# Two decode attentions on one core: VectorE and ScalarE programs as loops over chunk pairs, B's output weights loaded straight into one small buffer

## The chip, the cores and the metric

One core of one Trainium2 chip. The metric is device microseconds of one execution. The changed kernel and the kernel before were run alternately on one chip; executions of one kernel agree within about 0.2%.

## The reference, cut to what matters

```python
# two problems, A and B; 4 sequences, one query each, head size 128, bf16
# A: 32 query heads share 8 key/value heads; the last 2048 keys count
# B: 32 heads with keys and values of their own; 8192 keys
def ref(x, k_cache, v_cache, wq, wo):
    q = (x @ wq).reshape(B, Sq, H, Dh).transpose(0, 2, 1, 3)
    scores = einsum("bhqd,bhkd->bhqk", q, k) * Dh ** -0.5
    o = einsum("bhqk,bhkd->bhqd", softmax(scores), v)
    return o.transpose(0, 2, 1, 3).reshape(B, Sq, H * Dh) @ wo
# out = concatenate([A, B], -1)
```

Every key and value is used once: 587 MB come from memory, nine tenths of them B's.

## The kernel before

Work is cut into 8 chunks of A (2 MB of keys, 2 MB of values) and 64 of B (one sequence, two heads: 4 MB of keys, 4 MB of values). For each chunk PE transposes the keys in groups of 8 tiles, DVE and ACT copy them out of PSUM, PE multiplies them with the query, then softmax and the product with the values follow. SP issues all loads, in order. A small scheduler writes a list of operations for each engine; only PE's list is turned into a loop over pairs of B chunks, with waits against `i * step + value`.

```python
def emit_looped(self, engname, eng, sems, loop):
    a, b, steps = self.periods()              # where PE's list repeats
    self.emit_ops(pe[:m[a]], eng, sems)
    with loop(0, b - a) as i:
        self.emit_ops(pe[m[a]:m[a + 1]], eng, sems,
                      lambda sname, val: i * steps[sname] + val if steps[sname] else val)
    self.emit_ops(pe[m[b]:], eng, sems)
# ... (cut)
@block.tensor                                  # PE: a loop
def _(e): sch.emit_looped("pe", e, sems, loop)
@block.vector                                  # DVE and ACT: every instruction written out
def _(e): sch.emit("dve", e, sems)
@block.scalar
def _(e): sch.emit("act", e, sems)
# ... (cut) output weights: 512 KB (4 heads) into one of three slots; DVE copies the 2 heads in use
def dma_wo(i):
    dst = wor[:, slot, :].rearrange("p (hl n) -> p hl n", hl=4)
    sch.add_dma("sp", lambda e: e.dma_start(dst, src), "d_wo%d" % slot, waits=waits, key=("wo", i))
def emit_wos(c):
    sch.add("dve", lambda e: e.tensor_copy(wos[:, :, :], w[:, h:h + 2, :]), ...)
```

PE needs the same operands in each turn of its loop, hence the small copy `wos`.

## Time and profile before

| | before |
|---|---|
| time, median of 6 runs | 1386.33 us (1384.96 to 1387.15) |
| read from memory | 587.2 MB, 424 GB/s over the span, 431 in the steady stage |
| busy PE, DVE, ACT | 85%, 46%, 31% of the span |
| PE's wait for keys | 169 us in 61 waits |
| instructions run; written out for PE, DVE, ACT | 57,099; 3453, 1328, 526 |

### The profile page before, as it was taken

To read this page: it belongs to the slowest core of one execution; us is meant where nothing else is said; L and a number is where in the kernel's file an instruction comes from. 1 tells how busy PE (TensorE), PEld (TensorE's weight loads), DVE (VectorE), ACT (ScalarE), POOL (GpSimd) and SP (SyncE) were. 2 spreads that over 40 slices of the span, in tenths; PEclk is the share of its full clock that TensorE was granted. 3 is DMA by queue.
4 is the path that set the end of the run, shared out by engine and by line. 5 is a ranking of instruction groups with operands and counts; after the bars stand their busy time and mean duration, and the time that the engine had idled before them with its cause. 6 is when DMAs were issued, how large, how long until landed. Compare 5 with 4: busy or idle time off the path is not lost.

```text
span 1384.5 us, 57099 instructions
## 1 busy us (share of the span) xinstructions
PE 1173.0 (85%) x26769; PEld 1130.0 (82%) x26769; DVE 643.2 (46%) x1326; ACT 436.1 (31%) x649; POOL 4.1 (0%) x14
## 2 busy tenths in 40 slices
PE   4888888898888788988889788888898888888888
PEld 4777878897888788887889788887798888887887
DVE  1566444454444444444444444444454445444443
ACT  1554323333223322332233233332233233322332
POOL 1000000000000000000000000000000000000000
PEclk9899999999999999999999999999999999999998
DMA  9999999999999999999999999999999999999996
GB/s 400 414 417 422 426 428 430 434 425 437 427 436 427 432 430 434 429 425 436 427 436 427 435 427 436 426 428 435 429 434 430 433 427 435 428 429 432 431 434 255
DMA packets 29979, 587.80 MB, mean 425 GB/s; under 512 B 2656, under 2 KB 10864, under 8 KB 11120
## 3 DMA queue, kind: packets, MB, share of 16 engines
q1 hardware_dynamic: 29912, 587.22, 99.2%
q8 instruction: 27, 0.44, 0.1%
q14 instruction: 16, 0.13, 0.0%
q10 hardware_dynamic: 24, 0.01, 0.0%
HBM read 587.21 MB, written 0.01 MB: 424 GB/s over the span
## 4 chain that ended last, share of the span: by engine, by line
DMA 66%; PE 31%; DVE 1%; issue 1%; ACT 0%; SPq 0%; ACTq 0%; DVEq 0%
DMA kv<-in_B_k_cache_dram 64%; PE tr L321 19%; PE sc L323 9%; DMA kv<-in_B_wq_dram 2%; PE fin L323 2%; PE po L323 1%; PE ms L323 1%; DVE sA L430 1%; DVE kt L383 0%; DVE rm L439 0%; DVE sA L428 0%; ACT pba L493 0%; PE ms L321 0%; ACT kt L381 0%; ACT pbb L478 0%
## 5 line engine op out<-in xcount | busy, mean ns | idle before, releaser
L321 PE MATMUL tr<-identb,kv 128*128 128x128 bf16 x8704 | 702.7, 231 | 171.7 <-DMA kv<-in_B_k_cache_dram 169.0
L383 DVE COPY kt<-tr 128x1024 bf16<-128x1024 bf16 x736 | 502.6, 691 | 484.5 <-PE tr L321 480.4
L321 PEld LDWEIGHTS tr<-identb,kv 128*128 128x128 bf16 x8704 | 557.7, 105 | 197.4 <-issue 128.6
L381 ACT ACTIVATE kt<-tr 128x1024 bf16<-128x1024 bf16 x352 | 360.2, 1024 | 638.1 <-PE tr L321 635.0
L323 PE MATMUL sc<-qb,kt 128*128 128x64 bf16 x8192 | 424.6, 197 | 1.7 <-issue 1.5
L323 PEld LDWEIGHTS sc<-qb,kt 128*128 128x128 bf16 x8192 | 350.8, 101 | 3.9 <-issue 1.6
L323 PE MATMUL po<-pbb,kv 128*128 128x64 bf16 (+1 forms) x8192 | 289.9, 192 | 5.5 <-issue 5.5
L323 PEld LDWEIGHTS po<-pbb,kv 128*128 128x128 bf16 x8192 | 263.3, 97 | 7.6 <-issue 5.8
L478 ACT ACTIVATE pbb<-sc,negb 64x128 bf16<-64x128 f32 x128 | 51.2, 400 | 296.8 <-DVE negb L468 296.0
L444 DVE TENSOR_REDUCE rm<-sc 64x1 f32<-64x128 f32 x128 | 37.0, 289 | 94.2 <-PE sc L323 93.3
L456 DVE TENSOR_REDUCE gm<-ms 1x2 f32<-1x128 f32 (+1 forms) x72 | 20.1, 279 | 44.6 <-PE ms L321 44.5
L468 DVE COPY negb<-ms 128x1 f32<-128x1 f32 (+1 forms) x72 | 11.4, 159 | 55.4 <-PE ms L323 55.4
L323 PE MATMUL sc<-qs,kt 128*128 128x64 bf16 (+3 forms) x512 | 26.6, 198 | 10.8 <-DVE kt L383 10.5
L323 PEld LDWEIGHTS sc<-qs,kt 128*128 128x128 bf16 x512 | 21.8, 102 | 13.2 <-DVE kt L383 11.8
L323 PE MATMUL ms<-identf,gx 1*128 1x1 f32 (+1 forms) x144 | 27.8, 260 | 0.6 <-DVE gx L460 0.6
L323 PEld LDWEIGHTS ms<-identf,gx 1*128 1x128 f32 (+1 forms) x144 | 21.7, 188 | 4.9 <-DVE gx L460 0.8
L478 ACT ACTIVATION_READ_ACCUMULATOR pbb<-sc,negb 64x1 f32 x128 | 23.7, 185 | 0.0
L321 PE MATMUL ms<-identf,rm 128*1 128x128 f32 (+1 forms) x72 | 19.8, 275 | 0.2 <-DVE rm L444 0.2
L323 PE MATMUL fin<-wos,oz 128*4 128x512 bf16 x64 | 19.5, 386 | 0.3 <-DVE oz L542 0.3
L323 PE MATMUL po<-pba,kv 128*128 128x64 bf16 x512 | 18.9, 193 | 0.0
L460 DVE TENSOR_SCALAR gx<-gm 1x128 f32<-1x128 f32 (+1 forms) x72 | 15.9, 221 | 2.5
L323 PEld LDWEIGHTS po<-pba,kv 128*128 128x128 bf16 x512 | 16.6, 98 | 0.0
(47 smaller groups left out, 155.5 us busy)
## 6 DMA issues: line engine op xcount, KB each, us to landing
kv<-in_B_k_cache_dram SPq DMA_DIRECT2D x64, 4096.0 KB, 27.7
kv<-in_B_v_cache_dram SPq DMA_DIRECT2D x63, 4096.0 KB, 32.5
kv<-in_A_k_cache_dram SPq DMA_DIRECT2D x8, 2048.0 KB, 27.4
kv<-in_A_v_cache_dram SPq DMA_DIRECT2D x8, 2048.0 KB, 26.6
kv<-in_A_wq_dram SPq DMA_DIRECT2D x1, 4096.0 KB, 12.3
kv<-in_B_wq_dram SPq DMA_DIRECT2D x1, 4096.0 KB, 27.3
wor<-in_A_wo_dram SPq DMA_DIRECT2D x8, 512.0 KB, 23.6
wor<-in_B_wo_dram SPq DMA_DIRECT2D x8, 512.0 KB, 33.6
```

The costliest lines, as they stand in the source:

```text
L321: emit = lambda e: e.transpose(o, l, r)
L323: emit = lambda e: e.matmul(o, l, r, start=start, stop=stop)
L381: sch.add("act", lambda e: e.activation(dst, src, ACTF.Copy), waits=waits, key=("ev", s))
L383: sch.add("dve", lambda e: e.tensor_copy(dst, src), waits=waits, key=("ev", s))
L430: emit = lambda e, src=src, b=b: e.scalar_tensor_tensor(out=t, in0=src, scalar=mk[:, b:b + 1], in1=t, op0=ALU.mult, op1=ALU.add)
L444: sch.add("dve", lambda e, src=src, pp=pp: e.tensor_reduce(out=rm[pp, m, 0:1], in_=src, axis=AX.X, op=ALU.max), waits=[("S", ch["s_last"]) ...
L456: sch.add("dve", lambda e: e.tensor_reduce(out=gm[0:C, m, 0:U], in_=src, axis=AX.X, op=ALU.max), waits=[("trm", c)], key=("gmax", c))
L460: sch.add("dve", lambda e: e.tensor_scalar(out=dst, in0=gv, scalar1=-scale, scalar2=None, op0=ALU.mult), waits=[("gmax", c)], key=("gx", c))
L468: sch.add("dve", lambda e: e.tensor_copy(negb[:, m, 0:C], ms[:, col:col + C]), waits=[("bc", c)], key=("negb", c))
L478: sch.add("act", lambda e, src=src, pp=pp, n=n, u=u: e.activation(pbv[pp, :, u], src, ACTF.Exp, bias=negb[pp, m, 0:1], scale=scale, accum_ ...
```

## The change: intent and diff

The intent: shorter VectorE and ScalarE programs (1328 to 295 and 526 to 122 instructions written out), by the same loop that PE has. A loop's turns must be alike, which the three slots and the alternating masks of before were not. So B's output weights now go by DMA straight into `wos`, 256 KB for each head pair, and a mask multiplication replaces the two result buffers.

```diff
-        rz = sb("rz", [P, 2, 8], F32)
+        rz = sb("rz", [P, 8], F32)
+        pm = sb("pm", [P, HB // 2, 2, 2, 4], F32)          # 0/1 masks for the two pairs of a head pair
@@
+        def dma_wos(hp):
+            src = B_wo[2 * hp * P:2 * (hp + 1) * P, :].rearrange("(hl d) n -> d hl n", d=P)
+            sch.add_dma("sp", lambda e: e.dma_start(wos[:, :, :], src), "d_wos",
+                        waits=[("fin", NCA + 4 * hp - 1)] if hp else [], key=("wos", hp))
@@ SP's list
+            if kind == "k" and c >= NCA and (c - NCA) % 4 == 3:
+                dma_wos((c - NCA) // 4)
             dma_kv(kind, c)
+            if kind == "v" and c > NCA + 2 and (c - NCA) % 2 == 1:
+                sch.add("sp", lambda e: e.sem_inc(sems["eng_sp"], 1), waits=[("wos", (c - NCA - 2) // 4)], ...)
@@ after the reciprocal of a B pair
+                sch.add("dve", lambda e, x=0: e.tensor_tensor(out=rz..., in0=bcast(ri, ...),
+                    in1=pv[:, bass.ds(x + pair, 8)]..., op=ALU.mult), waits=[("rinv", c), "c_pm"], ...)
@@
-        def emit_wos(c): ...                                # the copy on DVE
@@ output product of a pair
-                if c > NCA + 2 and (c - NCA) % 2 == 1 and g == 4:
+                if c > NCA + 2 and (c - NCA) % 2 == 1 and g == 10:
                     emit_fin(c - 2)
@@
-            sch.emit("dve", e, sems)
+            sch.emit_looped("dve", e, sems, loop_on(mybir.EngineType.DVE, 0), 1)
-            sch.emit("act", e, sems)
+            sch.emit_looped("act", e, sems, loop_on(mybir.EngineType.Activation, 0), 1)
```

(Cut: the search for the period for each engine, and addresses that advance with the turn.)

More of the change, by code (lines that the diff above doesn't have):

```diff
@@ L25, with __getattr__, call, of @@
 TRM0, BC0, L0, Q0, XT0 = 0, 256, 288, 320, 448
+class _Record:
+    def __getattr__(self, name):
+        def call(*args, **kw):
+            return (name,) + tuple(self.of(x) for x in args) + tuple((k, self.of(kw[k])) for k in sorted(kw))
+        return call
+    @staticmethod
+    def of(x):
+        if isinstance(x, bass.AP):
+            return x.tensor.name, x.offset, str(x.ap), str(x.dtype)
+        return str(x)
 class _Sched:
@@ L36, in __init__, with add @@
         self.marks = []
-    def add(self, eng, emit, waits=(), key=None, what=None):
+    def add(self, eng, emit, waits=(), key=None, at=None, self_inc=False):
         sig = None
@@ L44, in add @@
             self.tk[key] = ("eng_" + eng, self.count[eng])
-        self.ops[eng].append((emit, tuple(waits), sig, what))
+        self.ops[eng].append((emit, tuple(waits), None if self_inc else sig, at))
     def add_dma(self, eng, emit, semname, waits=(), key=None):
@@ L55, in mark @@
     def mark(self):
-        self.marks.append(len(self.ops["pe"]))
+        self.marks.append({n: len(self.ops[n]) for n in self.ops})
     def needs(self, waits):
@@ L65, in needs, with emit_ops @@
         return need
-    def emit_ops(self, ops, eng, sems, value=lambda sname, val: val):
+    def emit_ops(self, ops, eng, sems, step=None, count=None):
         waited = {}
-        for emit, waits, sig, _ in ops:
+        for k, (emit, waits, sig, at) in enumerate(ops):
             for sname, val in self.needs(waits).items():
@@ L72, in emit_ops @@
                     continue
-                eng.wait_ge(sems[sname], value(sname, val))
+                by = step[sname] if step else 0
+                eng.wait_ge(sems[sname], count * by + val if by else val)
                 waited[sname] = val
-            ins = emit(eng)
+            if at is None:
+                ins = emit(eng)
+            else:
+                ins = emit(eng, count * step[k] if step else 0)
             if sig is not None:
@@ L80, in emit, with periods @@
         self.emit_ops(self.ops[engname], eng, sems)
-    def periods(self):
-        pe, best = self.ops["pe"], (0, 0, {})
-        for a in range(len(self.marks) - 1):
-            steps, b = {}, a
-            first = pe[self.marks[a]:self.marks[a + 1]]
-            while b + 1 < len(self.marks):
-                this = pe[self.marks[b]:self.marks[b + 1]]
-                if len(this) != len(first) or any(x[2:] != y[2:] for x, y in zip(first, this)):
-                    break
-                fine = True
-                for x, y in zip(first, this):
-                    nx, ny = self.needs(x[1]), self.needs(y[1])
-                    fine = fine and set(nx) == set(ny)
-                    for sname in set(nx) & set(ny):
-                        if b > a:
-                            fine = fine and ny[sname] - nx[sname] == (b - a) * steps.setdefault(sname, (ny[sname] - nx[sname]) // (b - a))
+    def periods(self, engname, pairs):
+        ops, marks = self.ops[engname], [m[engname] for m in self.marks]
+        rec = _Record()
+        says = [(emit(rec) if at is None else emit(rec, -at), sig) for emit, _, sig, at in ops]
+        best = (0, 0, {})
+        for a in range(len(marks) - pairs):
+            w0, w1 = marks[a], marks[a + pairs]
+            n, step = 1, {}
+            while a + (n + 1) * pairs < len(marks):
+                v0, v1 = marks[a + n * pairs], marks[a + (n + 1) * pairs]
+                fine = says[w0:w1] == says[v0:v1]
+                for k in range(w1 - w0 if fine else 0):
+                    x, y = self.needs(ops[w0 + k][1]), self.needs(ops[v0 + k][1])
+                    if ops[w0 + k][3] is not None:
+                        x[k], y[k] = ops[w0 + k][3], ops[v0 + k][3]
+                    fine = fine and set(x) == set(y)
+                    for c in set(x) & set(y):
+                        fine = fine and y[c] - x[c] == n * step.setdefault(c, (y[c] - x[c]) // n)
@@ L99, in periods @@
                 if not fine:
                     break
-                b += 1
-            if b - a > best[1] - best[0]:
-                best = (a, b, steps)
-        return best
-    def emit_looped(self, engname, eng, sems, loop):
-        a, b, steps = self.periods()
-        assert b - a > 2 and all(v >= 0 for v in steps.values()), (a, b, steps)
-        pe, m = self.ops[engname], self.marks
-        self.emit_ops(pe[:m[a]], eng, sems)
-        with loop(0, b - a) as i:
-            self.emit_ops(pe[m[a]:m[a + 1]], eng, sems, lambda sname, val: i * steps[sname] + val if steps[sname] else val)
-        self.emit_ops(pe[m[b]:], eng, sems)
+                n += 1
@@ new lines, in periods, with emit_looped @@
+            if n > best[1]:
+                best = (a, n, step)
+        return best
+    def emit_looped(self, engname, eng, sems, loop, pairs):
+        a, n, step = self.periods(engname, pairs)
+        assert n > 2 and all(v >= 0 for v in step.values()), (engname, a, n, step)
+        ops, m = self.ops[engname], [x[engname] for x in self.marks]
+        self.emit_ops(ops[:m[a]], eng, sems)
+        with loop(0, n) as i:
+            self.emit_ops(ops[m[a]:m[a + pairs]], eng, sems, step, i)
+        self.emit_ops(ops[m[a + n * pairs]:], eng, sems)
@@ L142, in bass_concat_heads__sliding_block_cached__mha_block_cached__decode_kernel @@
     for g in range(Hkv):
-        chunks.append(dict(ab=0, U=NB, C=REP, g=g, wo=g, NT=NB * W // P, norm=g, last=True, n0=0))
+        chunks.append(dict(ab=0, U=NB, C=REP, g=g, NT=NB * W // P, norm=g, last=True, n0=0))
     for hp in range(HB // 2):
         for b in range(NB):
-            chunks.append(dict(ab=1, U=2, C=1, hp=hp, b=b, wo=Hkv + hp // 2, NT=2 * SkB // P,
+            chunks.append(dict(ab=1, U=2, C=1, hp=hp, b=b, NT=2 * SkB // P,
                                norm=Hkv + hp, last=b == NB - 1, n0=2 * b))
@@ L159, in bass_concat_heads__sliding_block_cached__mha_block_cached__decode_kernel @@
     assert sum(LASTV) == NTB and NTA * 16 == 1024 and NTB * 2 <= 512 - NW
-    wo_last = {}
-    for c, ch in enumerate(chunks):
-        wo_last[ch["wo"]] = c
-    wo_first = {}
-    for c, ch in enumerate(chunks):
-        wo_first.setdefault(ch["wo"], c)
-    NWOL = len(wo_last)
-    NP = (NC - NCA) // 2
     sch = _Sched()
@@ L212, in bass_concat_heads__sliding_block_cached__mha_block_cached__decode_kernel @@
         xtps = ms[:, XT0:XT0 + KC * NB].bitcast(BF16)
-        semnames = ["eng_pe", "eng_dve", "eng_act", "eng_pool", "d_x0", "d_x1", "d_o0", "d_o1"]
+        semnames = ["eng_pe", "eng_dve", "eng_act", "eng_pool", "eng_sp", "d_x0", "d_x1", "d_o0", "d_o1"]
         semnames += ["d_h%d" % i for i in range(NH)] + ["d_vl%d" % i for i in range(len(LASTV))]
-        semnames += ["d_wo%d" % i for i in range(NWO)]
+        semnames += ["d_wo%d" % i for i in range(NWO)] + ["d_wos"]
         sems = {n: es.enter_context(nc.semaphore(n)) for n in semnames}
@@ L230, in bass_concat_heads__sliding_block_cached__mha_block_cached__decode_kernel @@
         sch.add("pool", lambda e: e.memset(qb[:, :, :], 0.0), key="c_qb")
-        sch.add("pool", lambda e: e.memset(rz[:, :, :], 0.0), key="c_rz")
+        sch.add("pool", lambda e: e.memset(pm[:, :, :, :, :], 0.0), key="c_pm0")
+        for x in range(2):
+            sch.add("pool", lambda e, x=x: e.memset(pm[:, :, x, x, :], 1.0), waits=["c_pm0"], key="c_pm" if x else None)
         sch.add("pool", lambda e: e.memset(pbt[0][:, :, :], 0.0), key=("c_pb", 0))
@@ L258, in dma_wq, with dma_wo @@
             sch.add_dma("sp", lambda e: e.dma_start(flat(at, 2), src), "d_h%d" % at, waits=waits, key=("wq", ab))
-        def dma_wo(i):
-            ab, wg = (0, i) if i < Hkv else (1, i - Hkv)
-            slot = i % NWO
-            src = WO[ab][wg * 4 * P:(wg + 1) * 4 * P, :].rearrange("(hl d) n -> d hl n", d=P)
-            dst = wor[:, slot, :].rearrange("p (hl n) -> p hl n", hl=4)
-            waits = [("wos" if i - NWO >= Hkv else "fin", wo_last[i - NWO])] if i >= NWO else []
-            sch.add_dma("sp", lambda e: e.dma_start(dst, src), "d_wo%d" % slot, waits=waits, key=("wo", i))
+        def dma_wo(g):
+            src = A_wo[g * 4 * P:(g + 1) * 4 * P, :].rearrange("(hl d) n -> d hl n", d=P)
+            dst = wor[:, g % NWO, :].rearrange("p (hl n) -> p hl n", hl=4)
+            sch.add_dma("sp", lambda e: e.dma_start(dst, src), "d_wo%d" % (g % NWO),
+                        waits=[("fin", g - NWO)] if g >= NWO else [], key=("wo", g))
+        def dma_wos(hp):
+            src = B_wo[2 * hp * P:2 * (hp + 1) * P, :].rearrange("(hl d) n -> d hl n", d=P)
+            sch.add_dma("sp", lambda e: e.dma_start(wos[:, :, :], src), "d_wos",
+                        waits=[("fin", NCA + 4 * hp - 1)] if hp else [], key=("wos", hp))
         def dma_kv(kind, c):
@@ L301, in bass_concat_heads__sliding_block_cached__mha_block_cached__decode_kernel @@
             loads.insert(2 * c + 1, ("v", c))
-        wo_next = 0
         for kind, c in loads:
+            if kind == "k" and c >= NCA and (c - NCA) % 4 == 3:
+                dma_wos((c - NCA) // 4)
             dma_kv(kind, c)
-            if kind == "v":
-                while wo_next < NWOL and wo_first[wo_next] <= c:
-                    dma_wo(wo_next)
-                    wo_next += 1
-        assert wo_next == NWOL
+            if kind == "v" and c > NCA + 2 and (c - NCA) % 2 == 1:
+                sch.add("sp", lambda e: e.sem_inc(sems["eng_sp"], 1), waits=[("wos", (c - NCA - 2) // 4)], key=("wos2", c - 2), self_inc=True)
+            if kind == "v" and c < NCA:
+                dma_wo(c)
+        sch.add("sp", lambda e: e.sem_inc(sems["eng_sp"], 1), waits=[("wos", HB // 2 - 1)], key=("wos2", NC - 1), self_inc=True)
         ms_read = []
@@ L316, in pe_mm @@
         def pe_mm(o, l, r, start=True, stop=True, transpose=False, waits=(), key=None):
-            def desc(x):
-                return x.tensor.name, x.offset, str(x.ap), str(x.dtype)
             if transpose:
-                emit = lambda e: e.transpose(o, l, r)
+                sch.add("pe", lambda e: e.transpose(o, l, r), waits, key)
             else:
-                emit = lambda e: e.matmul(o, l, r, start=start, stop=stop)
-            sch.add("pe", emit, waits, key, what=(desc(o), desc(l), desc(r), start, stop, transpose, key is not None))
+                sch.add("pe", lambda e: e.matmul(o, l, r, start=start, stop=stop), waits, key)
         def emit_xT():
@@ L349, in emit_q @@
             if ab == 1:
-                src, dst = src.rearrange("p (h b) -> p h b", b=NB), dst.rearrange("p (b h) -> p h b", b=NB)
+                src, dst = src.rearrange("p (hp u b) -> p hp b u", b=NB, u=2), dst.rearrange("p (hp b u) -> p hp b u", b=NB, u=2)
             else:
@@ L388, in emit_qb @@
         def emit_qb(c):
-            col = NB * HQ + chunks[c]["b"] * HQ + 2 * chunks[c]["hp"]
-            sch.add("dve", lambda e: e.tensor_copy(qb[:, c % 2, 0:2], qs[:, col:col + 2]),
-                    waits=["c_qb", ("q", 1)] + ([("S", chunks[c - 2]["s_last"])] if c - 2 >= NCA else []), key=("qb", c))
+            col = NB * HQ + 2 * (c - NCA)
+            sch.add("dve", lambda e, x=0: e.tensor_copy(qb[:, c % 2, 0:2], qs[:, bass.ds(x + col, 2)]), at=col,
+                    waits=["c_qb", ("S", chunks[c - 2]["s_last"])] if c - 2 >= NCA else ["c_qb", ("q", 1)], key=("qb", c))
         def emit_S(s):
@@ L526, in norm_sum @@
             else:
-                bp = chunks[c]["b"] // 2
-                m, n, rs, ri = NSM, 4, rst[1][:, :], rz[:, bp, 4 * bp:4 * bp + 4]
+                m, n, rs, ri = NSM, 4, rst[1][:, :], rinv[:, 0, 0:4]
             pe_mm(ms[:, L0:L0 + n], onesf[:, :], rs, waits=[("rs", c), "c_onesf"] + ms_read, key=("L", c))
-            sch.add("dve", lambda e: e.reciprocal(out=ri, in_=ms[:, L0:L0 + n]), waits=[("L", c), "c_rz"], key=("rinv", c))
+            sch.add("dve", lambda e: e.reciprocal(out=ri, in_=ms[:, L0:L0 + n]), waits=[("L", c)], key=("rinv", c))
+            if chunks[c]["ab"] == 1:
+                pair = 4 * (c - NCA - 1)
+                pv = pm[:, :, :, :, :].rearrange("p a b c d -> p (a b c d)")
+                sch.add("dve", lambda e, x=0: e.tensor_tensor(
+                    out=rz[:, :].rearrange("p (x y) -> p x y", x=2), in0=bcast(ri, [[0, 2], [1, 4]]),
+                    in1=pv[:, bass.ds(x + pair, 8)].rearrange("p (x y) -> p x y", x=2), op=ALU.mult),
+                    waits=[("rinv", c), "c_pm"], key=("rz", c), at=pair)
             ms_read[:] = [("rinv", c)]
@@ L540, in norm_out @@
                 o, i0 = oz[:, :].rearrange("p (x y) -> p x y", x=2), bcast(po[:, 0:4], [[0, 2], [1, 4]])
-                i1 = rz[:, chunks[c]["b"] // 2, :].rearrange("p (x y) -> p x y", x=2)
-            sch.add("dve", lambda e: e.tensor_tensor(out=o, in0=i0, in1=i1, op=ALU.mult),
-                    waits=[("rinv", c), ("pv", c)] + ([("fin", c - 2)] if c >= 2 else []), key=("oT", c))
+                i1 = rz[:, :].rearrange("p (x y) -> p x y", x=2)
+            waits = [("rinv" if c < NCA else "rz", c), ("pv", c)] + ([("fin", c - 2)] if c >= 2 else [])
+            sch.add("dve", lambda e: e.tensor_tensor(out=o, in0=i0, in1=i1, op=ALU.mult), waits=waits, key=("oT", c))
             po_read[:] = [("oT", c)]
-        def emit_wos(c):
-            h = 2 * chunks[c]["hp"] % 4
-            w = wor[:, chunks[c]["wo"] % NWO, :].rearrange("p (hl n) -> p hl n", hl=4)
-            sch.add("dve", lambda e: e.tensor_copy(wos[:, :, :], w[:, h:h + 2, :]),
-                    waits=[("wo", chunks[c]["wo"])] + ([("fin", c - 2)] if c - 2 >= NCA else []), key=("wos", c))
         def emit_fin(c):
@@ L559, in emit_fin @@
                 ops = [(ov[:, :, u], wos[:, u, :]) for u in range(2)]
-                waits = [("oT", c), ("wos", c)]
+                waits = [("oT", c), ("wos2", c)]
             else:
-                w = wor[:, ch["wo"] % NWO, :].rearrange("p (hl n) -> p hl n", hl=4)
+                w = wor[:, c % NWO, :].rearrange("p (hl n) -> p hl n", hl=4)
                 ov = oT[:, c % NSM, :].rearrange("p (u c) -> p u c", c=REP)
                 ops = [(ov[:, :, cc], w[:, cc, :]) for cc in range(REP)]
-                waits = [("oT", c), ("wo", ch["wo"])]
+                waits = [("oT", c), ("wo", c)]
             lastc = NC - 1 if ab == 1 else NCA - 1
@@ L597, in keys_part @@
                     emit_fin(c - 2)
-                if c > NCA + 1 and (c - NCA) % 2 == 0 and g == 4:
-                    emit_wos(c - 1)
                 if c > NCA + 1 and (c - NCA) % 2 == 0 and g == 6:
                     norm_sum(c - 1)
-                if c > NCA + 2 and (c - NCA) % 2 == 1 and g == 4:
+                if c > NCA + 2 and (c - NCA) % 2 == 1 and g == 10:
                     emit_fin(c - 2)
@@ L639, in bass_concat_heads__sliding_block_cached__mha_block_cached__decode_kernel @@
         sch.mark()
-        emit_wos(NC - 1)
         norm_sum(NC - 1)
@@ L651, in _, with loop_on, loop @@
             e.wait_ge(sems["d_o1"], 16)
+        def loop_on(eng, slot=None):
+            def loop(first, end):
+                return nc.Fori(first, end, 1, engines=type(mybir.ALL_ENGINES)([eng]), head_slot=None if slot is None else {eng: slot})
+            return loop
         @block.tensor
         def _(e):
-            pe = mybir.EngineType.PE
-            def loop(first, end):
-                return nc.Fori(first, end, 1, engines=type(mybir.ALL_ENGINES)([pe]), head_slot={pe: 0})
-            sch.emit_looped("pe", e, sems, loop)
+            sch.emit_looped("pe", e, sems, loop_on(mybir.EngineType.PE, 0), 1)
         @block.vector
         def _(e):
-            sch.emit("dve", e, sems)
+            sch.emit_looped("dve", e, sems, loop_on(mybir.EngineType.DVE, 0), 1)
         @block.scalar
         def _(e):
-            sch.emit("act", e, sems)
+            sch.emit_looped("act", e, sems, loop_on(mybir.EngineType.Activation, 0), 1)
         @block.gpsimd
```

## The prediction

The forecast's sum came to 1386.41 - 0.2 = 1386.2 us. The count of 4 to 6 packets behind the 0.2 used a block size that was not shown; from the page alone, 27 packets for 3453 + 1328 + 526 = 5307 instructions written out, the 1437 fewer would be about 7 packets, 0.12 MB, 0.3 us at 431 GB/s (an estimate). The price of a register instruction in a loop was not shown either; that the loops add 0 to the path is the author's estimate.

> **What bounds the kernel now.** I read the page first (busy shares, the slices, the queues, the chain), then the waits, the windows by stage, the chain in order of time, and one chunk pair on the timeline.
>
> ```profile
> PE 1173.0 (85%) x26769; PEld 1130.0 (82%) x26769; DVE 643.2 (46%) x1326; ACT 436.1 (31%) x649; POOL 4.1 (0%) x14
> ...
> GB/s 400 414 417 422 426 428 430 434 425 437 427 436 427 432 430 434 429 425 436 427 436 427 435 427 436 426 428 435 429 434 430 433 427 435 428 429 432 431 434 255
> ...
> q1 hardware_dynamic: 29912, 587.22, 99.2%
> q8 instruction: 27, 0.44, 0.1%
> ...
> DMA 66%; PE 31%; DVE 1%; issue 1%; ACT 0%; SPq 0%; ACTq 0%; DVEq 0%
> ```
>
> PE looks busiest (85%), but the transfer row is flat at 425 to 437 GB/s from slice 5 to slice 39, and the chain of waits is 66% DMA. The program reads 587.2 MB once. The windows of the steady stage (columns: us, busy us and instructions of PE, PEld, DVE, ACT, POOL, then granted clock, DMA share, GB/s):
>
> ```profile
> 200.00:480.00 280.00, 241.74 (x5546) 235.06 (x5544) 130.89 (x266) 86.76 (x132) 0.00 (x0) 0.93 1.00 431
> 480.00:760.00 280.00, 242.81 (x5629) 236.15 (x5626) 132.64 (x267) 88.09 (x130) 0.00 (x0) 0.94 1.00 431
> ```
>
> 431 GB/s with the DMA engines full, and the same in both. A pair of B chunks is 4 loads of 4,194,304 bytes = 16.78 MB; 16.78 MB / 431 GB/s = 38.9 us. The chain in order of time (start us, length us) repeats just that:
>
> ```profile
> 424.76 27.73 DMA kv<-in_B_k_cache_dram
> 452.54 1.51 PE tr L321 x24
> 463.62 29.24 DMA kv<-in_B_k_cache_dram
> 492.90 1.51 PE tr L321 x24
> 503.98 27.72 DMA kv<-in_B_k_cache_dram
> ```
>
> 463.62 - 424.76 = 38.86 us for an ordinary pair, 503.98 - 463.62 = 40.36 us for one that also carries a 512 KB output-weight load: that load costs 1.50 us. The compute engines have room:
>
> ```profile
> ACT kt L381 <- PE tr L321: 635.0, 340, 17.0
> DVE kt L383 <- PE tr L321: 480.4, 444, 7.1
> ACT pbb L478 <- DVE negb L468: 296.0, 64, 9.3
> PE tr L321 <- DMA kv<-in_B_k_cache_dram: 169.0, 61, 6.0
> ```
>
> DVE and ACT wait for PE; PE waits for keys from memory, 169.0 / 61 = 2.8 us a chunk, 5.6 us a pair. SP issues each load long before it is used: 27.7 us from issue to landing for keys and 32.5 us for values (issue table), of which 9.7 us (4.19 MB / 431 GB/s) is the load itself. So some 18 us of older work is queued when a key load is issued; it can be issued that much later before the queue runs dry.
>
> [...]27 instruction packets with 0.44 MB are 16 KB each, far below the 57,099 instructions executed, so PE's existing loop isn't fetched again per turn.[...]
>
> **The change part by part.**
>
> *Loops.* DVE's static program falls from about 1328 to 295 instructions, ACT's from 526 to 122 (counted in the built order); PE's stays at about 3450. [...]some 4 to 6 of 27 packets, up to 0.1 MB. At 431 GB/s that is 0.1 to 0.2 us over the whole run. No row of the waits puts DVE or ACT idleness down to instruction issue beyond ACT's start, so no stall is removed.
>
> The price: DVE's body has about 36 register instructions a pair (32 register sums for the waits, 4 for addresses and constants), ACT's 12, and each a closing branch. [...]DVE is busy 130.9 us of 280, so 18.2 us of a 38.9 us pair, leaving 20.7 idle; ACT is idle for longer. In the densest stretch, the key chunk, PE makes a group each 0.68 us, DVE copies two of three in 1.37 us of each 2.04 and then waits 0.67[...]. On the path: 0.
>
> *Output weights.* The B weights go from 8 loads of 512 KB to 16 of 256 KB: the same bytes and the same 1 KB rows. I take the cost as proportional: 8 x 1.50 = 12.0 us before, 16 x 0.75 = 12.0 after. What moves is where: pairs alternate 38.9 and 39.6 instead of three of 38.9 and one of 40.4. Sum 0, +-0.5.
>
> *DVE work.* 32 copies from the large weight buffer at 418 ns go (13.4 us), 32 mask multiplications of 128x8 come; the existing 128x8 multiplication takes 167 ns, so 5.3 us. DVE busy becomes about 643.2 - 13.4 + 5.3 = 635. Off the path: 0. Pool gets three more small memsets at the start, under 1 us, before anything reads them: 0.
>
> *Waits on SP.* A weight load now waits for the previous pair's last output product, just ahead of a key load. That product moves from key group 4 to 10, 6 x 0.68 = 4.1 us later. In the pair that I read on the timeline it ran at 534.85, so would run at 538.9; the key load behind it was issued at 542.83 because it waits for the end of the transposes. So the new wait ends 3.9 us before an old one: 0. SP also waits once per weight load for its landing, after issuing the next but one value load (569.65 in that pair). The weights land before the key load behind them (landed 570.61, own transfer 9.7), so near 561, some 9 us before SP looks. The output product that needs SP's signal comes ten groups into the chunk that begins at 570.61, over 7 us after SP's signal: 0.
>
> *Tail.* From the last key landing (1358.65) to the end (1384.5) PE sets the time. The last weight copy on DVE (1375.98, 0.42 us) ended before ACT's exponentials; the new multiplication would follow the reciprocal at about 1377.7, while the output product waits for the last value product at 1380.8. Sum 0.
>
> Total: 1386.41 - 0.2 (instruction bytes) = 1386.2 us.
>
> **The rivals.**
>
> *A loop is fetched again at every turn.* [...]each of about 29 turns waits for a fetch behind full data queues. For: the queues are full. Against: [...]PE's loop already turns without it. Even 3 us a turn falls where PE waits 2.8 us for keys, and 5.6 us a pair are free; only what exceeds that counts. At 8 us a turn, 29 x 2.4 = 70 us slower. I give this 1%.
>
> *SP's new waits dry the DMA queue.* For: [...]the weight buffer is single. Against: the margins of 3.9, 9 and 7 us above and 18 us of queued work. If the queue did dry for 1 us per weight load: +16 us, 1402, still within 2%. I give some such loss 3%.
>
> *Eviction becomes the bound.* Register instructions would have to cost more than 0.3 us each in the key chunk (0.67 / 2). PE's 38 sums a pair in its present loop leave no gap between groups. 1%.
>
> *It gets faster because fewer instructions are fetched.* The bytes are 0.1% of the traffic, worth at most a microsecond. A 2% gain (28 us) would need about 12 MB less traffic; there is none.
>
> **Range and chances.** The three runs of before spread 0.9 us; placement of weights and start-up may move 1 to 2 us either way. I chose 1383.8 to 1389.0 for 8 in 10, with the longer side upward for the rivals. Faster by over 2%: 1%; within 2%: 97%; slower by over 2%: 2%.
>
> **What would show it.** Right: the chain of waits is still about 66% DMA; 431 GB/s in the steady windows; DVE near 635 us, or a little different where records of the loop differ; the weight copy gone; instruction packets near 22; pairs of 38.9 and 39.6 us; PE's wait for keys still near 169 us. Wrong: instruction packets growing by 29 or more (refetch); GB/s below 428 in the steady windows with SP waiting for the weights; PE waiting for DVE's or ACT's kt in tens of microseconds; or fewer GB/s with no wait, which would mean that the smaller weight loads cost more than proportionally.

## More of the kernel before

```profile
q14 instruction: 16, 0.13, 0.0%
```

It says that besides the 27 packets of queue 8, 16 packets of instructions came on another queue, with a share that rounds to nothing.

## The result

1383.89 us median (1381.51 to 1384.30, 6 runs) against 1386.33 us; ratio 0.9982, 95% interval 0.9969 to 0.9995. A ratio here is the mean time of one kernel's runs over that of the other's of the same rounds, so not quite the ratio of the medians. It is inside the predicted range, but at its very lower edge: 2.4 us were gained where 0.2 were forecast. Two later calls repeat it (0.9982 and 0.9980), so the surplus is real.

The page of the changed kernel, the lines that answer to those of before:

```profile
PE 1172.3 (85%) x26769; PEld 1130.3 (82%) x26769; DVE 639.2 (46%) x1326; ACT 435.9 (32%) x649; POOL 4.5 (0%) x16
...
GB/s 400 415 415 426 424 430 430 429 434 428 435 428 434 430 429 429 430 437 426 436 430 430 429 430 436 425 437 430 431 430 429 433 428 436 429 433 430 429 432 311
...
q1 hardware_dynamic: 30040, 587.22, 99.6%
q8 instruction: 27, 0.44, 0.1%
q14 instruction: 6, 0.05, 0.0%
...
DMA 61%; PE 36%; DVE 1%; issue 1%; ACT 0%; SPq 0%; ACTq 0%; DVEq 0%
```

Queue 8 still has 27 packets; queue 14 fell from 16 to 6. The windows of the steady stage, and PE's wait for keys:

```profile
200.00:480.00 280.00, 245.07 (x5638) 238.59 (x5639) 132.83 (x271) 88.67 (x134) 0.00 (x0) 0.93 1.00 431
480.00:760.00 280.00, 241.72 (x5594) 235.13 (x5592) 129.28 (x264) 86.18 (x128) 0.00 (x0) 0.93 1.00 431
```

```profile
PE tr L344 <- DMA kv<-in_B_k_cache_dram: 162.2, 59, 5.9
```

Still full DMA engines, still 431 GB/s, still PE waiting for keys. So where did time go? The landings of keys tell. In the chain of waits in order of time, PE's transposes of a chunk start when its keys have landed. First every fourth pair of before (start us, length us), then of the changed kernel:

```profile
413.68 1.51 PE tr L321 x24
...
570.61 1.51 PE tr L321 x24
...
727.54 2.42 PE tr L321 x24
...
884.96 2.74 PE tr L321 x24
...
1042.88 1.51 PE tr L321 x24
...
1200.77 1.51 PE tr L321 x24
...
1358.65 2.10 PE tr L321 x24
```

```profile
413.40 2.74 PE tr L344 x24
...
570.33 2.74 PE tr L344 x24
...
727.31 2.74 PE tr L344 x24
...
884.22 2.74 PE tr L344 x24
...
1041.19 2.74 PE tr L344 x24
...
1198.10 2.74 PE tr L344 x24
...
1355.06 1.51 PE tr L344 x24
```

The changed kernel goes at 156.9 to 157.0 us in four pairs, from first to last. The kernel before has 156.93 twice (413.68 to 727.54), then 157.42, 157.92, 157.89 and 157.88: in its second half something costs about 1 us in every four pairs. At the last landing it is 1358.65 - 1355.06 = 3.6 us behind. The rest of the two profiled spans' difference (1384.5 against 1379.4, 5.1 us) is after the last landing, 25.85 us against 24.34; more of that below.

**What falls in those stretches.** The trace has a record of each DMA packet (start, queue, bytes, duration), without the number of its DMA engine. The queue-14 packets of before in the steady stage are 8192 bytes each and come in two regular series: at 292, 427, 564, 699, 836, 971, 1109 and 1244 us, 136 us apart, in which VectorE executes 129 instructions (266 in the 280 us of the window 200:480), and at 334, 612, 886 and 1173 us, 280 us apart, in which ScalarE executes 132. (One at 570 us is in neither series; whose it is was not shown.) The runs below with one program written out confirm it: unrolled_dve has the first series alone, unrolled_act the second alone. In the changed kernel there is one between 200 and 1300 us, at 470, and every run below has that one as well. Around the packet at 971 us of before, one engine's packets follow one another like this:

```
start us   queue  bytes   took us
979.887      1    32768    1.215     data
981.099     14     8192    0.325     instructions
981.412      1    32768    1.875     data: 0.66 longer
983.284      1    32768    1.213     data
```

(These raw times count from an earlier zero, 11.3 us before the views'. The block times above are raw times less 10.3, so 1 us later than a view would have them.) The block holds the engine up by 983.284 - 981.099 - 1.212 = 0.97 us. All eight blocks of the first series do this (0.325 to 0.333 us, next packet 1.867 or 1.875); those of the second cost about 0.7 us (0.309 or 0.318, next packet 1.594). From raw time 250 us to the end there are 14,638 data packets of 32 KB; the 13 that took over 1.3 us are the 13 right behind these blocks.

**Why one engine's delay can reach the end.** Each 4 MB load is 128 packets of 32 KB and 16 of 4 bytes, one report for each of the 16 engines; 8 data packets of 1.213 us, one behind the other, are 9.7 us, the time of a load, so 8 go to each engine. A load has landed when the last of the 16 has reported: the key load that PE's transposes wait for until 727.54 us has 16 reports, the first at 720.65 and the last at 727.54. Sorting the 16 reports of each load gives the lead of 15 engines over the slowest. Some of them, in us, before the change (ordinary output worked out from the packet records; its times run up to 0.6 us after the views'):

```
load landed   leads over the slowest engine (largest, then the five smallest)
 346.2        6.94 ... 1.79  1.73  1.69  1.66  0.59   (another has 3.42)
 433.6        6.94 ... 1.79  1.72  1.69  1.66  0.59   (3.42 -> 2.46)    block at 427
 571.1        6.95 ... 1.70  1.66  1.53  ...   0.59   (2.46 -> 1.53)    block at 564
 708.6        6.97 ... 1.74  1.72  1.69  0.61  0.51   (1.49 -> 0.51)    block at 699
 846.6        7.49 ... 2.22  2.19  2.16  1.08  0.47   everyone +0.47    block at 836
 975.4        8.49 ... 3.20  3.18  3.14  2.07  1.46   everyone +0.99    block at 971
1113.8        9.50 ... 4.14  4.12  4.10  3.00  2.42   everyone +0.96    block at 1109
1250.8       10.51 ... 5.17  5.11  5.08  3.98  3.39   everyone +0.98    block at 1244
```

Leads hardly change by themselves: the largest was 6.94 us at 346 and at 434 us, the 1.79 us one stayed at 1.79. One engine loses 0.93 to 0.98 us at each VectorE block, 3.42 to 0.51, and no one notices. The next block makes it the slowest of the sixteen, 0.47 us behind the one that was, and from then on each block delays every load: 0.47 + 0.99 + 0.96 + 0.98 = 3.4 us. That is the 3.6 us at the last landing, but for the 0.3 that was there at 413 us. ScalarE's blocks come off an engine that keeps a lead of 4.5 us and more, and change nothing. In the changed kernel the smallest lead stays at 0.2 to 0.3 us from 266 us on, that of 4 us (VectorE's engine, going by the other runs) at 3.9 to 4.1.

That is the theory, **lead used up**: VectorE's blocks come through one and the same DMA engine, each holds it up by 0.97 us, and it costs nothing until that engine is the slowest. So far it is read from two profiles. The rivals: the **smaller weight loads** and their new place in the queue; **any fetch counts**, with its delay, whichever engine; the **tail**.

### The profile page after: what moved, and what is told of

Its sections match the earlier page's. It is cut to its first block, busy times and chain, and to the rows that moved or that the text cites. A ratio compares the mean times of both kernels' runs of the same rounds, so it can differ in the third digit from the quotient of the medians.

```text
span 1379.4 us, 58812 instructions
## 1 busy us (share of the span) xinstructions
PE 1172.3 (85%) x26769; PEld 1130.3 (82%) x26769; DVE 639.2 (46%) x1326; ACT 435.9 (32%) x649; POOL 4.5 (0%) x16
## 4 chain that ended last, share of the span: by engine, by line
DMA 61%; PE 36%; DVE 1%; issue 1%; ACT 0%; SPq 0%; ACTq 0%; DVEq 0%
DMA kv<-in_B_k_cache_dram 59%; PE tr L344 22%; PE sc L346 9%; DMA kv<-in_B_wq_dram 2%; PE po L346 2%; PE fin L346 2%; PE ms L346 1%; DVE sA L453 1%; DVE kt L406 0%; DVE rm L462 0%; DVE sA L451 0%; ACT pba L516 0%; PE ms L344 0%; ACT kt L404 0%; DVE outsb L593 0%
## 6 DMA issues: line engine op xcount, KB each, us to landing
wos<-in_B_wo_dram SPq DMA_DIRECT2D x16, 256.0 KB, 20.5
```

## The experiments

All compute the right result. The later runs came in four calls on four chips (4, 14, 3 and 6), each with before beside it, so medians are best compared within a call. In the table, blocks are packets of queue 14, and the last key landing is from the chain of waits of each profiled run.

| run | blocks | last key landing | median us | before, same call | ratio (95%) |
|---|---|---|---|---|---|
| before (first profile) | 16 | 1358.65 | 1386.33 | | |
| changed (first) | 6 | 1355.06 | 1383.89 | 1386.33 | 0.9982 (0.9969-0.9995) |
| changed_again | 6 | 1355.31 | 1383.15 | 1384.95 | 0.9982 (0.9968-0.9995) |
| unrolled_both | 17 | 1358.37 | 1386.41 | 1384.95 | 1.0011 (0.9997-1.0024) |
| unrolled_dve | 14 | 1358.54 | 1386.35 | 1384.95 | 1.0006 (0.9993-1.0020) |
| unrolled_act | 9 | 1355.07 | 1383.81 | 1384.95 | 0.9987 (0.9973-1.0001) |
| pad_unrolled | 25 | 1366.37 | 1394.33 | 1386.16 | 1.0060 (1.0047-1.0074) |
| pad_looped | 9 | 1355.18 | 1383.00 | 1386.16 | 0.9983 (0.9969-0.9997) |
| pad_act_unrolled | 19 | 1359.14 | 1385.52 | 1385.17 | 1.0001 (0.9987-1.0014) |
| pad_act_looped | 6 | 1355.14 | 1383.57 | 1385.17 | 0.9985 (0.9971-0.9999) |
| half_loop_dve | 10 | 1355.04 | 1383.00 | 1386.30 | 0.9973 (0.9960-0.9987) |
| changed_third | 6 | 1354.88 | 1383.34 | 1386.30 | 0.9980 (0.9967-0.9994) |

### Undo the loops, keep the rest

```diff
-            sch.emit_looped("dve", e, sems, loop_on(mybir.EngineType.DVE, 0), 1)
+            sch.emit("dve", e, sems)
-            sch.emit_looped("act", e, sems, loop_on(mybir.EngineType.Activation, 0), 1)
+            sch.emit("act", e, sems)
```

Both lines for unrolled_both, the first alone for unrolled_dve, the second alone for unrolled_act.

> The changed kernel with the VectorE and ScalarE loops written out again; weights and masks as changed. Theory (instruction fetches): each 8 KB block of VectorE's program is fetched by one and the same DMA engine and holds it up by 0.97 us; once that engine is the slowest, every block lengthens the run. The gain goes back: within 0.8 us of the kernel before (about 1386), queue 14 again near 16 packets instead of 6, and in the completions of the loads the other 15 engines' leads over the last grow by 0.97 us at late VectorE fetches. Rival (the smaller weight loads and their place in the queue give the gain): stays near 1384, ratio 0.998. Rival (the shorter tail with PE at full clock gives it): no telling; the last key landing would be as in the changed kernel, 1355, and not near 1358.6.

> VectorE written out again, ScalarE still a loop. Theory: as with both written out, about 1386 and within 0.8 us of the kernel before, since the engine that VectorE's blocks use is the one that becomes slowest; queue 14 near 13 packets. Rival (any fetch counts, spread over engines): half way, near 1385. Rival (weights): near 1384.

> ScalarE written out again, VectorE still a loop. Theory: ScalarE's four blocks go through an engine with 2 us or more of lead, so they cost nothing: as the changed kernel, 1383.9, ratio 0.998; queue 14 near 10 packets. Rival (any fetch counts): 1384.5 to 1385.

> The changed kernel once more on the chip of these runs, as the mark for the others: 1383.9 us and 0.998 of before, if the difference is not of the chip that it was first timed on; near 1.000 if it is.

Measured on one chip: 1386.41, 1386.35, 1383.81 and 1383.15 us. The last key landing in the chain of waits of unrolled_both, unrolled_dve and unrolled_act, in this order:

```profile
1358.37 1.51 PE tr L344 x24
```

```profile
1358.54 1.95 PE tr L344 x24
```

```profile
1355.07 2.74 PE tr L344 x24
```

With VectorE written out the landing goes back to 1358.4 or 1358.5, whether ScalarE loops or not; with ScalarE alone written out it stays at 1355.1. In the packet records of unrolled_both the pattern of before appears again: one engine's lead goes 4.76, 3.81, 2.89, 1.91, 0.92 at the blocks up to 699 us, and from 835 us everyone's leads grow by 0.06 to 0.09 at the first and by 0.97 to 0.99 at each further one. The weights cannot be the gain: unrolled_both has them as changed, and is not faster than before (1.0011). Its 1.5 us over the median of before of that call is not clear of noise. "Any fetch counts" falls with unrolled_act, whose three blocks more than the changed kernel moved the landing by nothing. The 1383.81 against 1383.15 of changed_again is within the spread of both (1383.18 to 1384.12, 1381.83 to 1383.45).

### More VectorE blocks, the same work in or out of a loop

```diff
                 todo[15] = lambda: emit_qb(nxt + 1)
+        # and then, at the end of each B chunk, when DVE is idle, 16 memsets of one column:
+                    sch.add("dve", lambda e, i=16 * (nxt % 2) + i: e.memset(padt[:, i:i + 1], 0.0))
```

pad_unrolled has both programs written out, pad_looped both loops.

> Both programs written out, and 16 memsets of one column more on VectorE at the end of each B chunk, when it is idle: about 1040 instructions, 8 more blocks of 128. Theory: the engine that fetches them is the slowest after its lead of some 3.4 us is used up, so most of 8 x 0.97 = 7.8 us are added to the written-out kernel's 1386: 1391 to 1394. Rival (fetched bytes count only by their share of the traffic): 66 KB at 431 GB/s is 0.15 us: 1386. Rival (the memsets themselves delay PE): then the loop with the same memsets would be slower too.

> The same 16 memsets a chunk in the looped kernel, where they are executed as often[...]. Theory: as the changed kernel, 1383.9, within 0.8 us. Rival (executing them costs): as much slower than the changed kernel as the written-out one with them is over the written-out one without.

pad_unrolled took 1394.33 us, pad_looped 1383.00. Its queue 14 and its last key landing:

```profile
q14 instruction: 25, 0.20, 0.0%
```

```profile
1366.37 2.74 PE tr L345 x24
```

Eight more blocks than unrolled_both (25 - 17) put the landing 1366.37 - 1358.37 = 8.0 us later: 1.0 us a block, with 7.8 expected. The median is 7.9 us higher, or 6.7 when each is set against before of its own call. By the rule of bytes those 66 KB would be worth 0.15 us. The same memsets in the loop cost nothing, with 9 blocks fetched in all. The times of 1391 to 1394 that I gave allowed for some of the blocks to be free; in fact the blocks of unrolled_both had already used the lead up.

### More ScalarE blocks

```diff
                 sch.tk[("rs", c)] = sch.tk[("exp", c)]
+                for i in range(20):       # after the exponentials of each B chunk
+                    sch.add("act", lambda e, i=20 * (c % 2) + i: e.activation(padt[:, i:i + 1], mk[:, 0:1], ACTF.Copy))
```

pad_act_unrolled: VectorE looped, ScalarE written out with these. pad_act_looped: both looped.

> VectorE looped, ScalarE written out and with 20 one-column copies more at the end of each B chunk: 1280 instructions, 10 more blocks of 128, 14 over the steady stage with the 4 that are there. In the run with ScalarE alone written out each such block took 0.6 to 0.75 us, mean 0.71, off the lead of one engine, which had 5.8 us at 330 us. Theory (an engine costs nothing until its lead is used up): 14 x 0.71 - 5.8 = 4.1 us over the 1383.8 of that run: 1387.9, between 1386.5 and 1389. Rival (each block costs its 0.71 whatever the engine): 10 x 0.71 = 7.1 us: 1391. Rival (only VectorE's blocks can cost): 1383.8.

> The same 20 copies a chunk with both loops: executed as often[...]. Theory: as the changed kernel, 1383.2 to 1383.9. Rival (executing them delays the evictions): as slow as the written-out one.

Here the amount was missed. The median is 1385.52 us, 1.7 over unrolled_act and 2.0 over pad_act_looped of the same call, below the 1386.5 to 1389 that I gave. The profiled run itself took 1388.06, and its landing is where the theory had it, 1359.14 - 1355.07 = 4.07 us later:

```profile
1359.14 2.74 PE tr L345 x24
```

In its packet records one engine's lead falls by 0.7 at each ScalarE block, 4.10 at 295 us, 2.00 at 541 us, 0.68 at 727 us, 0.07 at 806 us, and then everyone's leads grow by 0.67 to 0.72 a block. So ScalarE's blocks cost as VectorE's do once the lead is gone, and the rival that only VectorE's can is out; so is the one that each costs at once (1391). But the other four runs, without records, took 1385.35 to 1386.85. A larger lead at the start could do that, but in the profiled runs the lead of this engine, going by its place in the order, differs by little over 1 us at 217 us (4.7 to 6.0). The tail after the landing differs by more (see Left open): with the shortest one that was seen, 24.4 us where this run had 26.8, the profiled run would have taken 1385.6, as three of the other four did. So the tail is the likelier cause, and the fault of my forecast is that it added up landings and left the tail out; this is argued, not shown. The copies in a loop cost nothing (1383.57).

### Only as many blocks as the lead covers

```diff
         a, n, step = self.periods(engname, pairs)
+        if engname == "dve":
+            a, n = a + 14, n - 14         # the first 14 pairs of the loop written out
```

> VectorE's loop begins 14 pairs later; the pairs before it are written out (813 instructions, about 7 blocks, of 295 and 1328). ScalarE looped. Theory (a lead is used up first): the four blocks that it fetches between 270 and 700 us come off the lead of their engine, 3.4 to 3.8 us in the earlier runs, and cost nothing, at most 0.5 us: last key landing at 1355.1 to 1355.6, time as the changed kernel of the same call. Rival (each block costs its share of the 3.3 us that the fully written-out VectorE lost at the last key landing): half of that, landing near 1356.7 and 1.2 to 1.6 us over the changed kernel.

> The changed kernel as the mark for the other: 1383 to 1384, last key landing at 1355.1 to 1355.4.

```profile
1355.04 2.74 PE tr L346 x24
```

VectorE fetched four blocks more than in the changed kernel (292, 428, 564, 709 us), and they cost nothing: landing 1355.04 against 1354.88, median 1383.00 against 1383.34. One engine's lead goes from 4.22 over 3.26, 2.30 and 1.37 to 0.44 us, and then there are no more blocks. Proportional cost would have put the landing near 1356.7. This is the run that speaks most directly for a lead that is used up: the same kind of block is free four times here and costs 1.0 us each time in pad_unrolled.

### Left open

What sets the leads at 220 us (two groups, 4 to 7 us and about 2 us ahead of the slowest) was not tried. The 26 packets of 16 KB on queue 8 between 19 and 236 us are a suspect that was not tested: each of them took 0.9 to 1.1 us. The **tail** after the last landing measured 24.3 to 27.0 us in the profiled runs, whichever kernel: 24.34 in changed, 24.43 in unrolled_both, 25.85 in before, 27.03 in pad_unrolled. It goes with the clock that PE was granted in it, and not with the change: 0.88 to 0.91 of full speed in the three profiled runs with 24.3 to 24.4 us, 0.83 to 0.86 in the six with about 25.9, 0.82 in the three with 26.8 to 27.0. So it is noise of the size of the effect. It may be why the medians differ by 1.8 to 3.0 us between changed and before in the three calls, where the landings differ by 3.3 to 3.8 (against the one profile of before); this is argued. No version was found that beats the changed kernel beyond noise: half_loop_dve is its equal.

## Why the prediction was right or wrong, point by point

- **The bound**: right. The DMA engines stay full, 431 GB/s, chain 61% DMA, PE waits 162 us for keys (169 foretold as unchanged).
- **Loops, fetched bytes**: this is the step that failed. "At 431 GB/s that is 0.1 to 0.2 us over the whole run" sized a block as if 16 engines shared it. An 8 KB packet runs on one engine: 0.33 us, plus 0.66 us on the packet behind it, 0.97 from start to start, against 8 KB / 431 GB/s = 0.02. Of the eight blocks removed in the steady stage, four were free, one cost half, three cost all: 3.4 us. The count was off too. I gave 27 packets to all engines and expected about 22; all 27 stayed. PE alone would account for them: of its 3453 written-out instructions nearly all are matrix products that run as two, a weight load and a multiplication, so about 6900 (26,769 of each were executed), 256 for each of the 27 packets, and queue 8 has 27 in every run, with VectorE and ScalarE in loops or written out. VectorE's and ScalarE's were on the line that I had skipped, among its 16 packets before and 6 after. "No stall is removed" was true of the engines' own waits, but the place to look was the DMA engines. That the first median fell inside the range, by 0.1 us, is luck: the two repeats (1383.15 and 1383.34) lie below it, and the room left downward was meant for placement and start-up.
- **Loops, price on the engines**: right that none of it reaches the path. 58,812 instructions were executed against 57,099; DVE's evictions in the key chunk are as close as before, and two in a row still take 1.37 us. What one register instruction costs was not shown. No block is fetched again in each turn: 6 packets on queue 14 with 29 turns.

```profile
538.63 1.37 DVE L406 COPY kt<-tr 128x1024 bf16<-128x1024 bf16 x2 [0.67 <-PE tr L344]
```

  (From the timeline of the changed kernel; the bracket is the idle time before and its releaser, as in before.)
- **Output weights**: right. Pairs alternate: landings at 256.44, 295.29, 334.90 and 373.77 us are 38.85, 39.61 and 38.87 us apart, where 38.9 and 39.6 were given; four pairs take 156.96 us against 156.93.
- **DVE's work**: right, within 4 us: 639.2 us against 635. The multiplication is 167 ns as assumed; some records of the small copies carry the loop's addresses and last 172 instead of 162 ns, and the groups of the wos copy are gone. Added up singly, VectorE's instructions fell by 7.8 us (662.3 to 654.5; 8.1 foretold); the busy time counts overlapping ones once and fell by 4.0. The new row:

```profile
L556 DVE TENSOR_TENSOR rz<-rinv,pm 128x8 f32<-128x8 f32 x32 | 5.4, 167 | 4.4 <-DVE rinv L552 0.2
```

- **Waits on SP**: right, with margins near those given. From the changed kernel's timeline of SP:

```profile
540.06 0.38 SPq L289 DMA_DIRECT2D wos<-in_B_wo_dram  x1
543.34 0.33 SPq L315 DMA_DIRECT2D kv<-in_B_k_cache_dram  x1
...
565.87 0.33 SPq L315 DMA_DIRECT2D kv<-in_B_v_cache_dram  x1
```

  The weights are issued 3.3 us before the key load that waits for something later anyway (3.9 foretold), land 20.5 us after issue in the median, near 560.6, and SP waits for them only after 565.87: 5 us to spare where I had 9. The output product ran at 580.17, 14 us after that. No load was held back.
- **Tail**: right that the change does nothing to it; I had not foreseen that it varies by 2.7 us by itself.
- **The rivals**: "It gets faster because fewer instructions are fetched" was worth "at most a microsecond" for me. It was the one that came, with 1.8 to 3.0 us in the medians and 3.3 to 3.8 at the landings, and it was put aside by the same misread share. The other three did not come.

## What to carry to other kernels

Here all 16 DMA engines are full (431 GB/s, DMA share 1.00) and every load waits for all of them. A small transfer on one engine then counted by the time that it took from that engine (0.97 us for 8 KB of VectorE's program, about 0.7 of ScalarE's), not by its bytes over the total rate (0.02 us). It was free while that engine was ahead of the slowest (four blocks in half_loop_dve), and once it was the slowest each one lengthened the run (1.0 us a block in pad_unrolled). So in a kernel with this picture, look at what else is on the DMA engines in the steady stage, program text too: loops took it from 16 packets to 6 here, and the last keys landed 3.6 us earlier.
